# Linear attention into a gated layer: neighbouring heads on the two partition halves, 128-partition loads, and a 136-column product

## The chip, the cores and the metric

One core of one Trainium2 chip runs one launch of the kernel. The metric is the device time of that launch in microseconds (us). With one core there is no second die to compare. The span of a profiled run is some 1.8 us shorter than its time on the clock, so spans are compared with spans and times with times. About 0.15%, or 0.45 us, is the noise between jobs; differences of steady chunks within traces repeat to 0.01 us.

## The reference, cut to what matters

```python
def _attn_ref(q, k, v):                       # each (8 batches, 8 heads, 576, 64), float32
    phi = lambda x: np.where(x > 0, x, np.exp(x) - 1.0) + 1.0
    q_p, k_p = phi(q), phi(k)
    kv  = np.einsum('bhsd,bhse->bhde', k_p, v)
    z   = np.sum(k_p, axis=2)
    num = np.einsum('bhsd,bhde->bhse', q_p, kv)
    den = np.einsum('bhsd,bhd->bhs', q_p, z)[..., None] + 1e-06
    return num / den
# x = attention output as (4608 tokens, 512);  w_in (512, 2048), w_out (2048, 512)
h = x @ w_in;  g = h - np.tanh(h);  out = g @ w_out
```

## The kernel before: the parts that matter

TensorE (PE) does the two large layers in chunks of 512 tokens: layer 1 (16 output tiles x 4 matmuls), then layer 2 (16 groups of 4). The attention of a later batch is threaded in as "steps" after the tiles (`s1`) and the groups (`s2`). Inputs are float32 in HBM; GpSimd's DMAs cast them to bf16.

```python
v_b = [const.tile([128, 2, 3, J, D], BF16) for i in range(2)]   # third "head" is all ones
def load_kq(b, src, store, name):          # batches 1 to 7: two DMAs of 64 partitions
    for hg in range(2) if b > 0 else ():
        nc.gpsimd.dma_start(out=t[64*hg:64*hg+64]..., in_=src[b, 4*hg:4*hg+4]...)
def kv_mm(b, i, ps):                       # per batch 36 matmuls, 64 rows, 192 columns
    nc.tensor.matmul(ps[hg], kp[r, i, j], vt[r, i, :, j, :], ...)   # 2 heads x 64 + 64 ones
attn = Banks([6, 7])                       # numerators alternate between two PSUM banks
def a_num(b, p):                           # numerator of head pair p, then its scaling
    ps = num_mm(b, p, attn)
    nc.vector.tensor_mul(xT[...], ps, rdb[...])
# order of the loads at the start:
#   q0 k0 v0 w_in(4 quarters) k1 q1 | w_out(0) w_out(1) v1 w_out(2)
# steps of batch 1 in chunk 0 (cut):
s1[9]  b0_scale_rest          s1[10] kphi  s1[12] kphi  s1[14] qphi      # layer 1
s2[1]  qphi, load q2, w_out(3), k2, v2     s2[2], s2[3] transposes of qp  # layer 2
s2[4]  prepare   s2[5] kv   s2[7] denominators   s2[8] numerators   s2[10], s2[12] spread
```

"qphi" is an exponential on ScalarE (ACT) and a max and a minimum on VectorE (DVE); its result, qp, is transposed on PE in chunk 0 and by DMA later. "kphi" is the same for k. gT is the gated output of layer 1, made on DVE from the tanh (th) of ACT. xT is the attention output after its scaling by the denominators, the input of layer 1; a "spread" copies the reciprocals of the denominators over the columns that they scale.

## Time and profile before

| | before |
|---|---|
| time, median of 3 runs | 298.7 us |
| span of the profiled run | 297.4 us |
| first matmul of layer 1 | 17.18 us |
| layer 2 of chunk 0 begins | 34.37 us |
| layer 1 of chunk 1 begins | 53.01 us |
| length of chunks 1 to 6, layer 1 to layer 1 | 30.77 us each |

Starts are read from the timeline of PE by line. A chunk's length is the distance between two starts of layer 1.

### The profile page before, as it was taken

How to read it: one execution, taken by the hardware profiler on the slowest of the kernel's cores; microseconds unless marked ns; L12 is line 12 of the kernel's file. 1: busy time of each engine (PE TensorE's matmuls, PEld its weight loads, DVE VectorE, ACT ScalarE, POOL GpSimd, SP SyncE). 2: the span in 40 equal slices, each digit the busy share in tenths (PEclk: the TensorE clock that was granted, in tenths of full speed). 3: DMA queues.
4: the chain of work that ended last, by engine and by line, in shares of the span. 5: the costliest groups of instructions: out<-in, count | busy, mean ns of one | idle time of the engine just before them, and what ended most of it. 6: DMA issues, size and time to landing. Idle time of an engine off the chain costs nothing.

```text
span 297.4 us, 4732 instructions
## 1 busy us (share of the span) xinstructions
PE 286.4 (96%) x1774; PEld 137.3 (46%) x1804; DVE 180.6 (61%) x317; ACT 149.5 (50%) x232; POOL 51.4 (17%) x89
## 2 busy tenths in 40 slices
PE   8898899999999999999999999999999999999994
PEld 3444354454445444544454445444544444444443
DVE  4759858886567764785478547855781468007600
ACT  3747816956444653465347525662562076136421
POOL 8952170240033002400060006000000000000000
PEclk9999999999999999999999999999999999999999
DMA  6999999898969666966797768887108310130033
GB/s 97 187 206 212 205 203 190 157 201 162 232 115 186 144 153 125 182 133 157 153 155 135 171 137 116 149 194 151 37 16 183 72 35 0 37 84 22 2 71 71
DMA packets 39126, 38.95 MB, mean 131 GB/s; under 512 B 16896, under 2 KB 33856, under 8 KB 38336
## 3 DMA queue, kind: packets, MB, share of 16 engines
q0 software_dynamic: 17600, 18.35, 38.8%
q1 hardware_dynamic: 21504, 20.31, 30.4%
q8 instruction: 14, 0.23, 0.3%
q14 instruction: 8, 0.07, 0.1%
HBM read 43.91 MB, written 9.55 MB: 180 GB/s over the span
## 4 chain that ended last, share of the span: by engine, by line
PE 86%; DMA 6%; POOL 5%; issue 1%; ACT 0%; POOLq 0%
PE ps_all L366 40%; PE ps_all L351 37%; DMA w_out_sb<-in_moe_w_out_dram 6%; PE ps_all L179 4%; PE ps_all L302 2%; PE ps_all L559 1%; POOL w_in_sb L113 1%; PE ps_all L259 1%; POOL qraw L88 1%; POOL v L107 1%; POOL kraw L88 1%; POOL v L391 1%; POOL kraw L92 0%; POOL qraw L92 0%; PE ps_all L166 0%
## 5 line engine op out<-in xcount | busy, mean ns | idle before, releaser
L351 PE MATMUL ps_all<-xT,w_in_sb 128*128 128x512 bf16 x560 | 127.3, 379 | 1.9 <-DVE xT L249 0.8
L366 PE MATMUL ps_all<-w_out_sb,gT 128*128 128x512 bf16 x547 | 125.8, 379 | 2.2 <-DMA w_out_sb<-in_moe_w_out_dram 1.3
L357 DVE TENSOR_TENSOR gT<-ps_all,th 128x512 bf16<-128x512 f32 x144 | 96.8, 686 | 50.7 <-ACT th L356 50.1
L356 ACT ACTIVATE th<-ps_all 128x512 f32<-128x512 f32 x144 | 85.0, 598 | 50.1 <-PE ps_all L351 45.2
L351 PEld LDWEIGHTS <-w_in_sb 128*128 128x128 bf16 x576 | 55.1, 98 | 67.6 <-issue 2.2
L366 PEld LDWEIGHTS <-gT 128*128 128x128 bf16 x560 | 54.0, 98 | 65.5 <-issue 1.8
L372 ACT COPY osb<-ps_all 128x512 f32<-128x512 f32 (+1 forms) x37 | 21.2, 573 | 77.5 <-PE ps_all L366 57.8
L313 DVE TENSOR_TENSOR xT<-ps_all,rdb 128x512 bf16<-128x512 f32 x24 | 16.5, 690 | 14.2 <-PE ps_all L302 14.2
L136 ACT ACTIVATE e<-qraw 128x1152 bf16<-128x1152 bf16 x16 | 18.7, 1167 | 4.5 <-DMA qraw<-in_q_dram 4.5
L107 POOL DMA_DIRECT2D v<-in_v_dram x32 | 19.4, 640 | 8.0 <-DMA w_in_sb<-in_moe_w_in_dram 4.0
L362 POOL COPY g<-gT 1x1 bf16<-1x1 bf16 x5 | 0.9, 177 | 111.5 <-DVE gT L357 111.5
L138 DVE TENSOR_TENSOR kp<-e,r 128x1152 bf16<-128x1152 bf16 x15 | 11.4, 758 | 13.3 <-ACT e L136 12.6
L136 ACT ACTIVATE e<-kraw 128x1152 bf16<-128x1152 bf16 x15 | 17.4, 1163 | 0.8 <-DMA kraw<-in_k_dram 0.8
L138 DVE TENSOR_TENSOR qp<-e,r 128x1152 bf16<-128x1152 bf16 x16 | 12.1, 758 | 7.6 <-ACT e L136 6.8
L179 PE MATMUL ps_all<-v,kp 64*128 64x192 bf16 x252 | 11.6, 243 | 0.0
L179 PEld LDWEIGHTS <-kp 64*128 64x128 bf16 x252 | 10.0, 94 | 3.0 <-issue 3.0
L416 PE MATMUL ps_all<-zero 128*128 128x512 bf16 x31 | 9.5, 469 | 1.2 <-DVE zero L379 1.2
L302 PE MATMUL ps_all<-qT,kz 128*128 128x512 bf16 x28 | 10.1, 379 | 0.1
L92 POOL DMA_DIRECT2D qraw<-in_q_dram x14 | 8.7, 639 | 6.2 <-DVE r L137 6.2
L92 POOL DMA_DIRECT2D kraw<-in_k_dram x14 | 8.7, 629 | 4.0 <-issue 2.7
L137 DVE TENSOR_SCALAR r<-qraw 128x1152 bf16<-128x1152 bf16 x16 | 7.5, 466 | 2.4 <-DMA qraw<-in_q_dram 2.4
L188 DVE TENSOR_TENSOR kz<-ps_all,mask 128x320 bf16<-128x320 f32 x14 | 6.2, 484 | 2.5 <-PE ps_all L179 2.5
(73 smaller groups left out, 97.9 us busy)
## 6 DMA issues: line engine op xcount, KB each, us to landing
out_dram<-osb SPq DMA_DIRECT2D x70, 128.0 KB
rdb<-ds SPq DMA_DIRECT2D x12, 576.0 KB
v<-in_v_dram POOLq DMA_DIRECT2D x32, 144.0 KB, 7.8
kraw<-in_k_dram POOLq DMA_DIRECT2D x14, 288.0 KB, 5.2
qraw<-in_q_dram POOLq DMA_DIRECT2D x14, 288.0 KB, 7.3
w_in_sb<-in_moe_w_in_dram POOLq DMA_DIRECT2D x4, 512.0 KB, 10.7
w_out_sb<-in_moe_w_out_dram POOLq DMA_DIRECT2D x4, 512.0 KB, 14.1
qraw<-in_q_dram POOLq DMA_DIRECT2D x4, 144.0 KB, 3.8
```

The costliest lines, as they stand in the source:

```text
L92: nc.gpsimd.dma_start(out=t[64 * hg:64 * hg + 64].rearrange("p i h j d -> p (i h) (j d)"), in_=src[b, 4 * hg:4 * hg + 4].rearrange("h (p j ...
L107: nc.gpsimd.dma_start(out=v_b[b % 2][64 * hg:64 * hg + 64, i, 0:2].rearrange("p h j d -> p h (j d)"), in_=v[b, h0:h0 + 2].rearrange("h (p ...
L136: return (lambda: nc.scalar.activation(e, x, AF.Exp), lambda: nc.vector.tensor_scalar(r, x, 0.0, 1.0, ALU.max, ALU.add), lambda: nc.vector ...
L138: lambda: nc.vector.tensor_tensor(y, e, r, ALU.min))
L179: nc.tensor.matmul(ps[hg], kp[r, i, j].rearrange("p h d -> p (h d)"), vt[r, i, :, j, :], start=(j == 0), stop=(j == J - 1))
L302: nc.tensor.matmul(ps, kz[:, p // 2, p % 2, 0:128], qT[:, p % 2, 0:8, p // 2, :], start=True, stop=True)
L313: nc.vector.tensor_mul(xT[:, p, S * b:S * b + 512].rearrange("p (j t c) -> p j t c", j=8, t=4), ps.rearrange("p j (t c) -> p j t c", t=4), ...
L351: nc.tensor.matmul(h, w_in_sb[:, p, fi * 128:(fi + 1) * 128], xT[:, p, c * 512:(c + 1) * 512], start=(n == 0), stop=(n == NP - 1))
L356: nc.scalar.activation(th, h, AF.Tanh)
L357: nc.vector.tensor_sub(gT[:, fi, :], h, th)
L366: nc.tensor.matmul(o, gT[:, fi, i * 128:(i + 1) * 128], w_out_sb[:, fi, :], start=(fi == 0), stop=(fi == NF - 1))
L372: nc.scalar.copy(osb[:, f0:f1], o[:, f0:f1])
```

## The change

The intent: with heads 2n and 2n+1 on the two partition halves, one DMA of 128 partitions loads what took two of 64. The rows of w_in have to follow. The 64 ones per pair of heads shrink to 8 in a separate tile `vp`, which VectorE fills from v. Chunk 0 is scheduled anew. Its core, with cuts:

```diff
+    kz_c = [const.tile([128, 2, 2, 160], BF16) ...]        # kz no longer from a pool
-    v_b = [const.tile([128, 2, 3, J, D], ...)]
+    v_b = [const.tile([128, 3, 2, J, D], ...)]
+    vp = const.tile([128, 2, J, 136], BF16, name="vp")
+    def load(b, t, src, halves):                            # q, k and v alike
+        x = src[b].rearrange("h (p j) d -> (h p) (j d)", j=J)
+        ... nc.gpsimd.dma_start(out=t..., in_=x.rearrange("(n q) x -> q n x", n=4))
     def load_wi(g):
-        nc.gpsimd.dma_start(out=w_in_sb[:, :, f0:f0 + DF // 4], ... "(ko ki) f -> ki ko f")
+        for h in range(2):
+            nc.gpsimd.dma_start(out=w_in_sb[64*h:64*h+64, ...], ... "(t d) f -> d t f")
+    def a_vp(b, i):
+        nc.vector.tensor_copy(vp[:, i, :, 0:128]..., v_b[b % 2][:, 0:2, i])
+    def a_kv_cols(b, banks):      # as a_kv, with vp[r, i, j, :]: 136 columns
     load_k(1)
+    load_wo(0)
     load_q(1)
-    load_wo(0)
     ...                           # prologue of batch 0: first half of qT, one of two copies moved off ACT;
                                  # second half, both moved onto it; fewer spins (matmuls on zeros)
-            s1[9].append(lambda: b0_scale_rest(first))
-            s1[10] kphi   s1[12] kphi   s1[14] qphi
+            s1[11] kphi   s1[13] kphi   s2[0] qphi
-            s2[2], s2[3] transposes  s2[4] prepare                   s2[5] kv  s2[7] ... s2[12]
+            s2[3], s2[4] transposes  s2[5] b0_scale_rest, prepare    s2[6] kv  s2[8] ... s2[13]
-            s1[...].append(lambda: a_kv(n1, attn))
+            s1[...].append(lambda: (a_kv if c == 1 else a_kv_cols)(n1, attn))
-            s2[d + 6].append(lambda: (a_qphi(n2, 1), a_qT_dma(n2)))
+            s2[d + 6].append(lambda: (a_qphi(n2, 1), a_qT_dma(n2), a_vp(n2, 0), a_vp(n2, 1)))
```

More of the change, by code (lines that the diff above doesn't have):

```diff
@@ L76 @@
     w_out_sb = const.tile([128, NF, DM], BF16, name="w_out_sb")
-    v_b = [const.tile([128, 2, 3, J, D], BF16, name=f"v{i}") for i in range(2)]
+    kz_c = [const.tile([128, 2, 2, 160], BF16, name=f"kz{i}") for i in range(2)]
+    v_b = [const.tile([128, 3, 2, J, D], BF16, name=f"v{i}") for i in range(2)]
+    vp = const.tile([128, 2, J, 136], BF16, name="vp")
     k_t, q_t = {}, {}
-    def load_kq(b, src, store, name):
-        t = kpool.tile([128, 2, 2, J, D], BF16, name=name)
-        for i in range(2) if b == 0 else ():
-            for hg in range(2):
-                h0 = 4 * hg + 2 * i
-                nc.gpsimd.dma_start(
-                    out=t[64 * hg:64 * hg + 64, i].rearrange("p h j d -> p h (j d)"),
-                    in_=src[b, h0:h0 + 2].rearrange("h (p j) d -> p h (j d)", j=J))
-        for hg in range(2) if b > 0 else ():
-            nc.gpsimd.dma_start(
-                out=t[64 * hg:64 * hg + 64].rearrange("p i h j d -> p (i h) (j d)"),
-                in_=src[b, 4 * hg:4 * hg + 4].rearrange("h (p j) d -> p h (j d)", j=J))
-        store[b] = t
+    def load(b, t, src, halves):
+        x = src[b].rearrange("h (p j) d -> (h p) (j d)", j=J)
+        if halves:
+            for i in range(2):
+                nc.gpsimd.dma_start(out=t[:, :, i].rearrange("q h j d -> q h (j d)"),
+                                    in_=x.rearrange("(h i q) x -> i q h x", h=2, i=2)[i])
+        else:
+            nc.gpsimd.dma_start(out=t.rearrange("q h i j d -> q (h i) (j d)"),
+                                in_=x.rearrange("(n q) x -> q n x", n=4))
@@ L97, in load_k @@
     def load_k(b):
-        load_kq(b, k, k_t, "kraw")
+        k_t[b] = kpool.tile([128, 2, 2, J, D], BF16, name="kraw")
+        load(b, k_t[b], k, b == 0)
     def load_q(b):
-        load_kq(b, q, q_t, "qraw")
+        q_t[b] = kpool.tile([128, 2, 2, J, D], BF16, name="qraw")
+        load(b, q_t[b], q, b == 0)
     def load_v(b):
-        for i in range(2):
-            for hg in range(2):
-                h0 = 4 * hg + 2 * i
-                nc.gpsimd.dma_start(
-                    out=v_b[b % 2][64 * hg:64 * hg + 64, i, 0:2].rearrange("p h j d -> p h (j d)"),
-                    in_=v[b, h0:h0 + 2].rearrange("h (p j) d -> p h (j d)", j=J))
+        load(b, v_b[b % 2][:, 0:2], v, b == 0)
@@ L111, in load_wi @@
     def load_wi(g):
         f0 = g * (DF // 4)
-        nc.gpsimd.dma_start(out=w_in_sb[:, :, f0:f0 + DF // 4],
-                            in_=moe_w_in[:, f0:f0 + DF // 4].rearrange("(ko ki) f -> ki ko f", ki=128))
+        for h in range(2):
+            nc.gpsimd.dma_start(out=w_in_sb[64 * h:64 * h + 64, :, f0:f0 + DF // 4],
+                                in_=moe_w_in[256 * h:256 * h + 256, f0:f0 + DF // 4].rearrange(
+                                    "(t d) f -> d t f", d=64))
     def load_wo(g):
@@ L126, in phi_pieces @@
             store[b] = work.tile([128, 2, J, 2, D], BF16, name=name)
-        x = src[b][:, i]
+        x = src[b][:, :, i]
         e = epool.tile([128, 2, J, D], BF16, name="e")
@@ L179, in kv_mm @@
                 nc.tensor.matmul(ps[hg], kp[r, i, j].rearrange("p h d -> p (h d)"),
-                                 vt[r, i, :, j, :], start=(j == 0), stop=(j == J - 1))
+                                 vt[r, :, i, j, :], start=(j == 0), stop=(j == J - 1))
     def a_kv(b, banks):
-        kz_t[b] = work.tile([128, 2, 2, 160], BF16, name="kz")
+        kz_t[b] = kz_c[b % 2]
         ps = [banks()[:, 0:384].rearrange("p (i e) -> p i e", i=2) for hg in range(2)]
@@ L188, in a_kv @@
             nc.vector.tensor_mul(kz_t[b][:, hg], ps[hg][:, :, 0:160], mask[:, hg])
+    def a_vp(b, i):
+        nc.vector.tensor_copy(vp[:, i, :, 0:128].rearrange("p j (h d) -> p h j d", h=2), v_b[b % 2][:, 0:2, i])
+    def a_kv_cols(b, banks):
+        kp = kp_t[b]
+        kz_t[b] = kz_c[b % 2]
+        ps = [banks()[:, 0:272].rearrange("p (i e) -> p i e", i=2) for hg in range(2)]
+        for i in range(2):
+            for j in range(J):
+                for hg in range(2):
+                    r = slice(64 * hg, 64 * hg + 64)
+                    nc.tensor.matmul(ps[hg][:, i, :], kp[r, i, j].rearrange("p h d -> p (h d)"),
+                                     vp[r, i, j, :], start=(j == 0), stop=(j == J - 1))
+        for hg in range(2):
+            nc.vector.tensor_mul(kz_t[b][:, hg, :, 0:136], ps[hg], mask[:, hg, :, 0:136])
     def b0_z(i):
@@ L195, in b0_z @@
                 r = slice(64 * hg, 64 * hg + 64)
-                nc.tensor.matmul(ps_all[:, 4 + 2 * i + hg, 0:32], kp_t[0][r, i, j].rearrange("p h d -> p (h d)"),
+                nc.tensor.matmul(ps_all[:, 4 - 2 * i + hg, 0:32], kp_t[0][r, i, j].rearrange("p h d -> p (h d)"),
                                  one[r, 0:32], start=(j == 0), stop=(j == J - 1))
     def b0_zc(i):
-        nc.vector.tensor_mul(kz_t[0][:, :, i, 128:160], ps_all[:, 4 + 2 * i:6 + 2 * i, 0:32], mask[:, :, i, 128:160])
+        nc.vector.tensor_mul(kz_t[0][:, :, i, 128:160], ps_all[:, 4 - 2 * i:6 - 2 * i, 0:32], mask[:, :, i, 128:160])
     def b0_kv(i):
@@ L207, in b0_kv @@
                 nc.tensor.matmul(ps_all[:, 2 * i + hg, 0:128], kp_t[0][r, i, j].rearrange("p h d -> p (h d)"),
-                                 v_b[0][r, i, 0:2, j, :], start=(j == 0), stop=(j == J - 1))
+                                 v_b[0][r, 0:2, i, j, :], start=(j == 0), stop=(j == J - 1))
     def b0_kz(i):
@@ L350, in l1mm @@
     def l1mm(c, fi, h, p, n):
-        nc.tensor.matmul(h, w_in_sb[:, p, fi * 128:(fi + 1) * 128], xT[:, p, c * 512:(c + 1) * 512],
+        nc.tensor.matmul(h, w_in_sb[:, 2 * (p % 2) + p // 2, fi * 128:(fi + 1) * 128], xT[:, p, c * 512:(c + 1) * 512],
                          start=(n == 0), stop=(n == NP - 1))
@@ L388 @@
     load_k(1)
+    load_wo(0)
     load_q(1)
     for i in (1, 0):
-        nc.gpsimd.memset(v_b[i][:, :, 2], 1.0)
-    load_wo(0)
+        nc.gpsimd.memset(v_b[i][:, 2], 1.0)
+    nc.gpsimd.memset(vp[:, :, :, 128:136], 1.0)
     load_wo(1)
@@ L418 @@
     side = Banks([4, 5, 6, 7])
-    kz_t[0] = work.tile([128, 2, 2, 160], BF16, name="kz")
+    kz_t[0] = kz_c[0]
     (eq0, rq0, mq0), (eq1, rq1, mq1) = (phi_pieces(0, q_t, qp_t, "qp", i) for i in range(2))
-    for f in (eq0, rq0, mq0, eq1, rq1):
+    for f in (eq0, rq0, mq0, eq1, rq1, mq1):
         f()
     spin(18)
-    a_qT_pe(0, 0, side, "AA")
+    a_qT_pe(0, 0, side, "AV")
     (ek0, rk0, mk0), (ek1, rk1, mk1) = (phi_pieces(0, k_t, kp_t, "kp", i, 2 * i) for i in range(2))
-    for f in (mq1, rk0, ek0):
+    for f in (ek0, rk0, *ek1, mk0, rk1):
         f()
-    spin(6)
-    a_qT_pe(0, 1, side, "VV")
-    for f in (*ek1, rk1, mk0):
-        f()
+    spin(5)
+    a_qT_pe(0, 1, side, "AA")
     for t in range(4):
@@ L436 @@
     nc.scalar.copy(sel, s8[:, 0].rearrange("q h p -> q p h").unsqueeze(3).to_broadcast([128, NP, 2, 64]))
-    spin(8)
+    spin(6)
     b0_z(0)
@@ L493, in num1 @@
                     a_num_copy(1, sub["ns"], p, side)
-            s1[9].append(lambda: b0_scale_rest(first))
-            s1[10].append(lambda: a_kphi(1, 0))
-            s1[12].append(lambda: a_kphi(1, 1))
-            s1[14].append(lambda: a_qphi(1, 0))
+            s1[11].append(lambda: a_kphi(1, 0))
+            s1[13].append(lambda: a_kphi(1, 1))
+            s2[0].append(lambda: a_qphi(1, 0))
             s2[1].append(lambda: (a_qphi(1, 1), load_q(2), load_wo(3), load_k(2), load_v(2)))
-            s2[2].append(lambda: a_qT_pe(1, 0, side))
-            s2[3].append(lambda: a_qT_pe(1, 1, side))
-            s2[4].append(prepare)
-            s2[5].append(lambda: a_kv(1, side))
-            s2[7].append(lambda: a_den(1, side))
-            s2[8].append(lambda: (num1(), a_split(1)))
-            s2[10].append(lambda: (spread1(0), a_qphi(2, 0)))
-            s2[12].append(lambda: (spread1(1), a_qphi(2, 1), a_qT_dma(2)))
+            s2[3].append(lambda: a_qT_pe(1, 0, side))
+            s2[4].append(lambda: a_qT_pe(1, 1, side))
+            s2[5].append(lambda: (b0_scale_rest(side), prepare()))
+            s2[6].append(lambda: a_kv(1, side))
+            s2[8].append(lambda: a_den(1, side))
+            s2[9].append(lambda: (num1(), a_split(1)))
+            s2[11].append(lambda: (spread1(0), a_qphi(2, 0)))
+            s2[13].append(lambda: (spread1(1), a_qphi(2, 1), a_qT_dma(2)))
             s2[15].append(lambda: a_kphi(2, 0))
         elif n1 < B:
-            s1[6 if c == 1 else 5].append(lambda: a_kv(n1, attn))
+            s1[6 if c == 1 else 5].append(lambda: (a_kv if c == 1 else a_kv_cols)(n1, attn))
             s1[9 if c == 1 else 8].append(lambda: (a_den(n1, attn), a_spread(n1)))
@@ L522 @@
             s2[d + 4].append(lambda: a_qphi(n2, 0))
-            s2[d + 6].append(lambda: (a_qphi(n2, 1), a_qT_dma(n2)))
+            s2[d + 6].append(lambda: (a_qphi(n2, 1), a_qT_dma(n2), a_vp(n2, 0), a_vp(n2, 1)))
         if c == 0:
-            first = Banks([4, 5, 6, 7, 0, 1, 2, 3, 2, 4, 5, 6, 7])
+            first = Banks([4, 5, 6, 7, 0, 1, 2, 3])
             hs = [ps_all[:, n, :] for n in range(4)]
```

## The prediction

> **What bounds the kernel now.** I read the page's head first, then the chain of waits, the PE waits, the stretch table, and single timelines.
>
> ```profile
> PE 286.4 (96%) x1774; PEld 137.3 (46%) x1804; DVE 180.6 (61%) x317; ACT 149.5 (50%) x232; POOL 51.4 (17%) x89
> ...
> DMA  6999999898969666966797768887108310130033
> ...
> PE 86%; DMA 6%; POOL 5%; issue 1%; ACT 0%; POOLq 0%
> ```
>
> TensorE is busy 286.4 of 297.4 us, and the chain that ended last is 86% PE. But the DMA row is at 9 from the second slice to the eighth: for the first 55 us the transfers are as full as PE. So there are two kernels in one: a start (0 to 53 us) where DMA and PE take turns, and a steady part where only PE counts. The stretch table (columns: PE, PEld, DVE, ACT, POOL busy; clock; DMA share; GB/s written) says so.
>
> ```profile
> 8.00:10.00 2.00, 1.50 (x11) 0.53 (x8) 1.28 (x3) 2.00 (x4) 2.00 (x4) 1.00 1.16 191
> 10.00:12.00 2.00, 2.00 (x16) 1.06 (x15) 1.82 (x5) 1.94 (x4) 2.00 (x4) 1.00 1.21 191
> ...
> 18.00:20.00 2.00, 2.00 (x24) 1.05 (x21) 1.28 (x2) 0.00 (x0) 0.00 (x0) 1.00 1.27 204
> 20.00:25.00 5.00, 5.00 (x25) 2.29 (x24) 3.35 (x6) 3.80 (x7) 1.35 (x2) 1.00 1.23 209
> 25.00:30.00 5.00, 4.19 (x23) 1.90 (x23) 4.35 (x8) 3.13 (x5) 1.73 (x3) 1.00 1.21 212
> ...
> 35.00:53.00 18.00, 17.63 (x153) 9.05 (x155) 12.78 (x32) 8.42 (x13) 5.58 (x9) 1.00 1.17 198
> ...
> 145.50:176.30 30.80, 30.64 (x186) 14.57 (x188) 20.49 (x33) 16.12 (x24) 5.02 (x9) 1.00 0.78 152
> ```
>
> A steady chunk takes 30.8 us with 0.16 us of PE idle: a nanosecond off PE there is a nanosecond off the kernel, and a new PE wait costs its full length. After the prologue PE waits little either:
>
> ```profile
> PE ps_all L366 <- DMA w_out_sb<-in_moe_w_out_dram: 1.3, 1, 1.3
> PE ps_all L351 <- DVE xT L249: 0.8, 1, 0.8
> ```
>
> **What the Trainium skill says.** "SBUF — State Buffer", Door 1: The DMA port swizzle: 64 partitions reach 8 of 16 ports and measured 196 GB/s at 1 MiB, against 328 for 128 partitions; this is presumably why the change was made. The trace does not bear it out here: the loads cast float32 to bf16, so written bytes are half the bytes read, and k and v of batch 0, 64 partitions each, were written at 191 GB/s (8 to 12 us), w_in at 128 partitions at 204 to 209, k and q of batch 1 at 64 partitions at 212. "DMA: Bandwidth & Descriptors", Rules for kernel authors, says two transfers to disjoint halves share the same 16 engines; that fits. "TensorE: Matmul & The Clock Gate", Back-to-back issue gap: warm, N/2.4 + 2.5 ns per matmul; the pairs below agree. "VectorE: DVE Perf Modes", The perf-mode tier table, puts bf16 tensor_copy and tensor_scalar in one 4x tier; so the new copies should cost what the tensor_scalar of the same 1152 elements costs (452 ns in the trace).
>
> **Part 1: kv with 136 columns instead of 192 (batches 3 to 7).** The v tile carried 64 ones per pair of heads, though the denominator needs a few columns. The timelines give 64x128 and 64x192 matmuls:
>
> ```profile
> 12.62 0.66 PE L207 MATMUL ps_all<-v,kp 64*128 64x128 bf16 x18
> ...
> 40.64 1.66 PE L179 MATMUL ps_all<-v,kp 64*128 64x192 bf16 x36
> ```
>
> Two row halves run together, so 18 matmuls are 9 pairs. Taking the last matmul's own time off: (660 - 216)/8 = 56 ns per pair at 128 columns, (1660 - 243)/17 = 83 ns at 192: 0.43 ns a column. At 136 columns about 59 ns. 18 pairs x 24 ns = 0.43 us a batch, 5 batches: **-2.1 us**, all on PE, all in stretches without PE slack.
>
> **Part 2: the copies into vp.** Two VectorE copies of 128x1152 bf16 a batch, 0.45 to 0.54 us each with spacing: 0.9 to 1.0 us, five times. VectorE has 10 us idle a chunk, so the sum is harmless; the place is not. They sit behind the last qp minimum and ahead of the first scaling of the numerators, and those numerators live in two PSUM banks:
>
> ```profile
> 139.33 0.76 DVE L138 TENSOR_TENSOR qp<-e,r 128x1152 bf16<-128x1152 bf16 x1 [1.11 <-ACT e L136]
> 140.00 1.36 DVE L313 TENSOR_TENSOR xT<-ps_all,rdb 128x512 bf16<-128x512 f32 x2
> ...
> 139.18 0.38 PE L302 MATMUL ps_all<-qT,kz 128*128 128x512 bf16 x1
> ...
> 140.25 0.38 PE L302 MATMUL ps_all<-qT,kz 128*128 128x512 bf16 x1
> ...
> 141.33 0.38 PE L302 MATMUL ps_all<-qT,kz 128*128 128x512 bf16 x1
> ```
>
> The third numerator (141.33) takes the bank that the first scaling must have read. That scaling now starts at 140.00. With 0.95 us of copies ahead it starts at 140.95, ends 0.69 later at 141.64; with some 0.06 us of signalling PE goes at 141.70: a new PE wait of about 0.37 us. It arises where copies and numerators are neighbours, in chunks 2 to 5 (in chunk 1 the numerators come two steps later): 4 x 0.37 = **+1.5 us** (0.6 to 2 for copies of 0.35 to 0.55 us).
>
> **Part 3: the loads at the start.** Twelve DMAs of 144 KB become six of 288 KB; w_in goes from four to eight. An issue takes about 0.63 us of GpSimd whether it covers 128 or 256 rows of the source, so q, k and v are issued in 6 x 0.64 instead of 12 x 0.64 us, 3.8 us less; w_in gives back about 4 x 0.65 = 2.6 less a little. But the queue is already backlogged: the first packets run at 2.5 us, and the k issued at 5.4 lands 5.7 us later. Bytes ahead of any weight stay equal. What is left is that q's first half is one request (it landed at 4.3 and 5.0 in two), with perhaps a better ramp (135 GB/s at 4 to 6 us against 191 later): I allow 0.5 us on all landings of the prologue, 0 to 1.2. The ACT and VectorE reordering (one qT copy moved off ACT before the k exponentials) does not win more by itself: the first w_in lands at 9.6 + 7.3 = 16.9 us, and the first L1 matmul ran at 17.2. So L1 starts near 16.5.
>
> **Part 4: the weights of chunk 0.** The first w_out quarter is moved ahead of q of batch 1. It landed at 17.2 + 17.2 = 34.4 us, where PE waited 1.3 us; 590 KB of written bf16 ahead of it at about 200 GB/s are 2.9 us, so it lands at about 31. The 0.8 us wait on xT (the rest of batch 0, moved into the second layer) goes too. L1 takes 64 x 0.216 = 13.8 us plus 0.5, so layer 2 starts near 31 instead of 34.4. But then PE runs into what comes next: q of batch 1, now behind, lands near 34, so its transposes can't run before 36; and the later quarters of w_out keep their place in the queue:
>
> ```profile
> 38.76 0.77 POOL L117 DMA_DIRECT2D w_out_sb<-in_moe_w_out_dram  x1
> ...
> DMA to landing us min/median/max: 9.3/9.3/9.3
> ```
>
> The last quarter landed at 38.8 + 9.3 = 48.1 us, and the step that needs it began at 49.4, after the spread at 48.2: only 1.3 us of slack. With everything 0.5 us earlier it lands at 47.6, when PE also arrives (second quarter at 36.4, then eight steps of 0.86 plus transposes, kv, denominators, numerators and spread, 4.3 us: 47.6). Four steps and one spread later, 3.9 us, layer 1 of chunk 1 begins at 51.5 against 53.2: **-1.7 us**, not the 3.4 that the start of layer 2 suggests.
>
> **Sum:** -2.1 + 1.5 - 1.7 = -2.3; I shade it to -2.6 for a better ramp: 298.7 - 2.6 = 296.1 us, 0.9% down.
>
> **The rivals.** (a) The 128-partition loads really are faster, as the port table says: then the eight DMA-full slices shrink, chunk 0 gains 4 us or more, and the time is 293 to 294. For it: the slow 4 to 8 us, all 64-partition loads. Against it: the 212 GB/s of later 64-partition loads, and w_in, which goes the other way. (b) The copies cause no PE wait (they are faster, or the minimum ahead comes earlier): then -2.1 - 1.7 gives 294.9. For it: only that the margin is small; against it the bank arithmetic above. (c) The copies run in a slower mode (0.76 us, as the minimum does): a wait of 1 us in four chunks, +4, and with -3.8 elsewhere the time stays near 299. (d) Chunk 0 gains nothing because the later q of batch 1 stalls the transposes and ACT, which carries the exponentials, the tanh and the copies in one order: the time is 298. ACT was busy all of 30 to 35 us, which speaks for some of it.
>
> **Range and chances.** The kv term is sure to 0.3 us; the copies' wait could be 0 to 4 us, chunk 0 could give 0 to 4 us. Combined, 8 in 10 lie in 293.8 to 298.2. Faster by 2% needs 292.7 or less, that is both rival a and rival b: 6%. Slower by 2% (304.7) has no mechanism: 1%. Within 2%: 93%.
>
> **What would show it.** A kv group of 64x136 matmuls near 1.2 us per 36; two copies near 0.45 us each; a PE wait on the scaling of xT of some 0.4 us in four chunks (none there means rival b); the first layer-1 matmul near 16.5 us and layer 2 of chunk 0 near 31; the last w_out quarter landing near 47.6 with PE waiting for it or just arriving; chunk 1 beginning near 51.5. Wrong would be: landings more than 1.5 us earlier throughout (a), or layer 1 still starting at 17 or later.

## The result, and the profile after

The changed kernel took 295.61 us (median of 4 runs, 295.37 to 295.89), the kernel before 298.86 us in 4 runs. The ratio is 0.9892, 95% interval 0.9875 to 0.9909. Ratios throughout are the mean time of one kernel's runs over that of the other's in the same rounds, so they are not quite the ratio of the medians quoted. That is 3.25 us less; 2.6 were predicted.

The head of the page after, against the one in the prediction:

```profile
PE 285.9 (97%) x1801; PEld 134.9 (46%) x1801; DVE 182.3 (62%) x326; ACT 150.4 (51%) x233; POOL 31.9 (11%) x53
...
DMA  6999999898959665957697679776117310230033
...
PE 91%; DVE 3%; DMA 3%; POOL 1%; issue 1%; ACT 0%; DVEq 0%; POOLq 0%
```

Before, GpSimd (POOL) stood at 51.4 us and 89 instructions; fewer DMAs bring it to 31.9 and 53, and its share of the chain that ended last falls from 5% to 1%. The DMA row is unchanged over the first 50 us. In that chain, DVE has come in with 3%. The waits of PE in the first 60 us (us in total, times, longest) lead to these DVE links:

```profile
PE ps_all L165 <- DVE qp L137: 1.2, 2, 0.6
PE ps_all L432 <- DVE zero L394: 1.2, 1, 1.2
PE ps_all L222 <- DMA v<-in_v_dram: 0.5, 1, 0.5
PE ps_all L366 <- DVE xT L245: 0.3, 1, 0.3
```

The two waits of before (1.3 us for w_out, 0.8 us for xT) are gone. A wait of transposes on qp has taken their place; of its two, one belongs to batch 0 at 7.7 us, and only 0.6 us to chunk 0. The chain from 29 to 35.8 us runs through DVE: products gT, both minima of k, then qp. The PE timeline of chunk 0 after shows the place:

```profile
31.59 3.62 PE L381 MATMUL ps_all<-w_out_sb,gT 128*128 128x512 bf16 x16
35.80 0.68 PE L165 MATMUL ps_all<-ident,qp 128*128 128x128 bf16 x9 [0.59 <-DVE qp L137]
...
51.12 2.10 PE L366 MATMUL ps_all<-xT,w_in_sb 128*128 128x512 bf16 x9
```

Layer 2 starts at 31.59 instead of 34.37, four groups (16 matmuls) run, PE waits for qp, and chunk 1 begins at 51.12 instead of 53.01. The later gain is in the products (groups of the page by line: busy us, mean ns) and in the steady stretch, whose PE idle is now rounded to nothing:

```profile
L200 PE MATMUL ps_all<-vp,kp 64*128 64x136 bf16 x180 | 6.2, 220 | 0.0
L190 DVE COPY vp<-v 128x1152 bf16<-128x1152 bf16 x10 | 4.1, 453 | 0.0
...
82.00:112.40 30.40, 30.40 (x192) 14.09 (x188) 21.29 (x36) 16.11 (x24) 2.40 (x4) 1.00 0.80 154
```

The busy sums would say 6.2/5 = 1.24 us a batch against 11.6/7 = 1.66: 0.42 us each. All times of the two profiled runs together:

| | before | after | difference |
|---|---|---|---|
| layer 1 begins | 17.18 | 16.94 | -0.24 |
| chunk 0, from there to layer 1 of chunk 1 | 35.83 | 34.18 | -1.65 |
| chunk 1 | 30.78 | 30.78 | 0 |
| chunks 2 to 5, each | 30.77 | 30.49 | 4 x -0.28 |
| chunk 6 | 30.77 | 30.36 | -0.41 |
| span | 297.4 | 294.0 | -3.4 |

Chunk 6 has the short product but no copies, chunks 2 to 5 have both: 0.41 us won, some 0.14 us given back. A timeline of chunk 2 after (DVE first, then PE) shows how:

```profile
106.25 0.76 DVE L137 TENSOR_TENSOR qp<-e,r 128x1152 bf16<-128x1152 bf16 x1 [1.10 <-ACT e L135]
106.92 0.82 DVE L190 COPY vp<-v 128x1152 bf16<-128x1152 bf16 x2
107.66 1.88 DVE L328 TENSOR_TENSOR xT<-ps_all,rdb 128x512 bf16<-128x512 f32 x3
```

```profile
106.09 0.38 PE L317 MATMUL ps_all<-qT,kz 128*128 128x512 bf16 x1
...
107.17 0.38 PE L317 MATMUL ps_all<-qT,kz 128*128 128x512 bf16 x1
...
108.39 0.38 PE L317 MATMUL ps_all<-qT,kz 128*128 128x512 bf16 x1
...
109.47 0.38 PE L317 MATMUL ps_all<-qT,kz 128*128 128x512 bf16 x1
```

Numerators come 1.08 us apart, except the third: 1.22 us, 0.14 too late. The first scaling began at 107.66 and took 0.69 us, so it ended at 108.35, and the third numerator, which needs its bank, began at 108.39. The profile does not list this as a wait, since PE is still counted busy with the tail of the matmuls before; only the spacing shows it.

### The profile page after: what moved, and what is told of

It is laid out like the page before. It is cut to its first block, busy times and chain, and to the rows that moved or that the text cites. A ratio compares the mean times of both kernels' runs of the same rounds, so it can differ in the third digit from the quotient of the medians.

```text
span 294.0 us, 4681 instructions
## 1 busy us (share of the span) xinstructions
PE 285.9 (97%) x1801; PEld 134.9 (46%) x1801; DVE 182.3 (62%) x326; ACT 150.4 (51%) x233; POOL 31.9 (11%) x53
## 3 DMA queue, kind: packets, MB, share of 16 engines
q1 hardware_dynamic: 21504, 20.31, 30.6%
## 4 chain that ended last, share of the span: by engine, by line
PE 91%; DVE 3%; DMA 3%; POOL 1%; issue 1%; ACT 0%; DVEq 0%; POOLq 0%
PE ps_all L366 42%; PE ps_all L381 40%; DMA v<-in_v_dram 3%; PE ps_all L317 2%; PE ps_all L200 2%; PE ps_all L572 1%; PE ps_all L178 1%; DVE gT L372 1%; PE ps_all L274 1%; DVE kp L137 1%; PE ps_all L241 1%; POOL kraw L90 0%; POOL qraw L90 0%; PE ps_all L222 0%; PE ps_all L165 0%
## 5 line engine op out<-in xcount | busy, mean ns | idle before, releaser
L381 PE MATMUL ps_all<-w_out_sb,gT 128*128 128x512 bf16 x560 | 128.1, 379 | 0.0
L328 DVE TENSOR_TENSOR xT<-ps_all,rdb 128x512 bf16<-128x512 f32 x24 | 15.8, 686 | 11.7 <-PE ps_all L317 11.7
L432 PE MATMUL ps_all<-zero 128*128 128x512 bf16 x29 | 8.6, 454 | 1.2 <-DVE zero L394 1.2
L285 DVE RECIPROCAL rden<-den 128x144 f32<-128x144 f32 x7 | 7.4, 1053 | 0.2
L136 DVE TENSOR_SCALAR r<-kraw 128x1152 bf16<-128x1152 bf16 x15 | 6.8, 451 | 0.1
L93 POOL DMA_DIRECT2D qraw<-in_q_dram x7 | 5.2, 748 | 14.6 <-DVE r L136 13.4
L200 PEld LDWEIGHTS <-kp 64*128 64x128 bf16 x180 | 5.3, 94 | 2.1 <-issue 2.1
L200 PE MATMUL ps_all<-vp,kp 64*128 64x136 bf16 x180 | 6.2, 220 | 0.0
L93 POOL DMA_DIRECT2D kraw<-in_k_dram x7 | 5.2, 749 | 3.7 <-issue 1.3
```

The lines of the kernel that those rows point to most:

```text
L93: nc.gpsimd.dma_start(out=t.rearrange("q h i j d -> q (h i) (j d)"), in_=x.rearrange("(n q) x -> q n x", n=4))
L136: lambda: nc.vector.tensor_scalar(r, x, 0.0, 1.0, ALU.max, ALU.add),
L200: nc.tensor.matmul(ps[hg][:, i, :], kp[r, i, j].rearrange("p h d -> p (h d)"), vp[r, i, j, :], start=(j == 0), stop=(j == J - 1))
L328: nc.vector.tensor_mul(xT[:, p, S * b:S * b + 512].rearrange("p (j t c) -> p j t c", j=8, t=4), ps.rearrange("p j (t c) -> p j t c", t=4), ...
L381: nc.tensor.matmul(o, gT[:, fi, i * 128:(i + 1) * 128], w_out_sb[:, fi, :], start=(fi == 0), stop=(fi == NF - 1))
```

## The experiments

My theory before the first runs: the steady part gives 1.5 us (shorter products less the bank wait), chunk 0 and its start give the rest, by order and schedule and not by the width of the loads. The main rival: the 128-partition loads do it.

### Products of 192 columns again

```diff
- s1[...]: (a_kv if c == 1 else a_kv_cols)(n1, attn)     s2[d+6]: ..., a_vp(n2, 0), a_vp(n2, 1)
+ s1[...]: a_kv(n1, attn)                                s2[d+6]: ...
```

> The changed kernel with the 136-column product and its two copies taken out again (all batches multiply the 192-column tile, as before). My theory: of the 3.25 us won, the steady part gives 5 x 0.42 us of shorter products less 4 x 0.14 us of a new PE wait, 1.5 us; so this kernel is 1.5 us slower than the changed one, about 297.1 us, ratio to before 0.994, with steady chunks of 30.77 us and chunk 1 still beginning near 51.3 us. Rival: the steady part wins nothing and all comes from the start; then 295.6 us, ratio 0.989.

Measured: 297.19 us (5 runs), ratio 0.9945 (0.9931 to 0.9958); chunks 1 to 6 are 30.77 us again, and chunk 1 begins at 51.03. Against the changed kernel that is 1.6 us. The steady part's share is settled, and 1.6 us are left for the start. In this profiled run PE waited 0.43 us for the last w_out quarter (landed at 47.2), and chunk 0 took 34.67 us; nothing in the edit touches that load.

### Copies behind the last numerator

```diff
- s2[d+6]: a_qphi(n2, 1), a_qT_dma(n2), a_vp(n2, 0), a_vp(n2, 1)
+ s2[d+6]: a_qphi(n2, 1), a_qT_dma(n2)      s2[14]: a_vp(n2, 0)      s2[15]: a_vp(n2, 1)
```

> The changed kernel with the two vp copies moved behind the last numerator of the chunk. Theory: the copies delay the first scaling of the numerators, so the third numerator waits for its PSUM bank (0.14 us in chunks 2 to 5); without them ahead the wait goes, 0.56 us less in all: 295.0 us, ratio 0.987, third numerator 1.08 us after the second. Rival: the spacing has another cause (the copies are free); then 295.6 us and the gap of 1.22 us stays.

Measured: 294.67 us (4 runs), ratio 0.9863 (0.9849 to 0.9876). Chunks 2 to 5 are 30.36 us, and the numerators are 1.08 us apart throughout. The DVE timeline of chunk 2 now reads:

```profile
105.74 0.76 DVE L137 TENSOR_TENSOR qp<-e,r 128x1152 bf16<-128x1152 bf16 x1 [1.10 <-ACT e L135]
106.42 1.36 DVE L328 TENSOR_TENSOR xT<-ps_all,rdb 128x512 bf16<-128x512 f32 x2
...
110.56 0.82 DVE L190 COPY vp<-v 128x1152 bf16<-128x1152 bf16 x2
```

The same two copies, at a place where DVE has nothing to do for PE, cost nothing. The chunks account for 4 x 0.14 = 0.56 us; the 0.9 us between the medians contain the noise between jobs.

### The copies twice

```diff
- s2[d+6]: ..., a_vp(n2, 0), a_vp(n2, 1)
+ s2[d+6]: ..., a_vp(n2, 0), a_vp(n2, 1), a_vp(n2, 0), a_vp(n2, 1)
```

> The changed kernel with the two vp copies done twice at the same place (the second pair rewrites the same values). Theory: two more copies at 0.37 us spacing push the first scaling back 0.74 us, and since the slack is already used up, the third numerator waits all of it, in chunks 2 to 5: 4 x 0.74 = 3.0 us more, 298.6 us, ratio 0.999. Rival: VectorE has 9 us idle a chunk, so copies cost nothing: 295.6 us.

Measured: 298.59 us (4 runs), ratio 0.9995 (0.9981 to 1.0008). Chunks 2 to 5 take 31.23 us, 0.74 more than in the changed kernel, chunk 1 is unchanged. Now the wait is long enough to be listed:

```profile
140.14 0.38 PE L317 MATMUL ps_all<-qT,kz 128*128 128x512 bf16 x1 [0.72 <-DVE xT L328]
```

VectorE is idle for about a third of a chunk, and yet 0.74 us of work in the wrong place costs 0.74 us each time, 4 x 0.74 = 3.0 us: nearly all of the change's gain.

### Loads of q, k and v by 64 partitions, everything else as changed

```diff
- nc.gpsimd.dma_start(out=t.rearrange("q h i j d -> q (h i) (j d)"), in_=x.rearrange("(n q) x -> q n x", n=4))
+ for g in range(2):            # same tiles, same rows, same order
+     nc.gpsimd.dma_start(out=t[64*g:64*g+64]..., in_=...)
```

> The changed kernel with every load of q, k and v cut in two DMAs of 64 partitions each, same tiles, same order, same bytes. My theory: PE is not waiting for these transfers in the changed kernel but for one DMA of v (0.5 us) and for qp; 64 or 128 partitions moves the landings by some 0.3 us, so 295.6 to 296.1 us, ratio 0.989 to 0.991. Rival (the 128-partition loads are what makes the start faster): the landings of the later weights slip back by the 1.2 to 1.6 us that they came earlier, and the time is 297 us or more, ratio 0.994 or more.

Measured: 296.06 us (4 runs), ratio 0.9913 (0.9899 to 0.9926). Next to the changed kernel's two series (295.61 and 295.22) that is 0.45 to 0.85 us. The last w_out quarter lands at 38.2 + 9.3 = 47.4 us, against 37.4 + 9.1 = 46.5 with 128 partitions. So the wide loads do make the landings about 0.9 us earlier, but most of this is not on PE's path: what reaches it is qp, for which PE now waits 0.9 us instead of 0.6. The rival's 1.4 us or more are refuted; my "0 to 0.5 us" was at its upper edge. The edit makes the DMAs twice as many as well as narrower, and the run does not tell the two apart.

### w_in by four DMAs of 128 partitions (wrong result on purpose)

```diff
- for h in range(2): nc.gpsimd.dma_start(out=w_in_sb[64*h:64*h+64, ...], ...)
+ nc.gpsimd.dma_start(out=w_in_sb[:, :, f0:f0 + DF // 4], ... "(ko ki) f -> ki ko f")
```

> The changed kernel with w_in loaded by four DMAs of 128 partitions again instead of eight of 64. Rows then meet the wrong tokens, so the result is wrong on purpose; times and traces are those of a valid kernel. My theory: w_in is not waited for once the first quarter is there, and 64 partitions are no slower here; 295.6 us give or take 0.4, ratio 0.988 to 0.991. Rival (64 partitions cost w_in bandwidth): 128 partitions are faster, 294.9 us or less, w_in landing 1 us or more earlier.

Measured: 295.68 us (4 runs), ratio 0.9896 (0.9875 to 0.9917); the result is wrong, as intended. The quarters of w_in land at 16.1, 19.5, 22.0 and 24.6 us; in halves of 64 partitions the later halves landed at 16.6, 19.4, 22.0 and 24.4. The first quarter is whole 0.5 us earlier, but the first matmul of layer 1 waits for xT and not for it; the later quarters agree within 0.2 us. For w_in, partition width makes no difference to the time that a run here shows.

### The w_out quarter behind q again

```diff
- load_k(1); load_wo(0); load_q(1)
+ load_k(1); load_q(1); load_wo(0)
```

> The changed kernel with the first w_out quarter behind q of batch 1 again, as before. Layer 2 of chunk 0 then begins when that quarter lands, near 33.2 us instead of 31.6. Theory: the two orders trade one wait for another: with q early, PE no longer waits 1.2 us for qp at the transposes, so only 0.4 us of the 1.6 us reach the end: 296.0 us, ratio 0.990. Rival: the order of these two loads carries the gain of chunk 0, and all 1.6 us come back: 297.2 us, ratio 0.9945.

Measured: 297.04 us (6 runs, 296.71 to 298.55), ratio 0.9956 (0.9933 to 0.9979). My 0.4 us is wrong. Two things had gone into it. First, I had read 1.2 us of waiting for qp off the list shown above, of which only 0.6 belongs to chunk 0; with the right figure 1.6 - 0.6 = 1.0 us is expected, and the four runs at full clock (296.71 to 297.11) show 1.1 to 1.5 over 295.61, or 1.5 to 1.9 over the 295.22 of the changed kernel's second series. The rival's 1.6 us fits no worse. The trade itself did not happen either. q landed at 30.6 us instead of 33.1, but qp came no earlier, as DVE shows (the changed kernel first, then this run):

```profile
33.23 1.28 DVE L372 TENSOR_TENSOR gT<-ps_all,th 128x512 bf16<-128x512 f32 x2
...
34.98 0.76 DVE L137 TENSOR_TENSOR qp<-e,r 128x1152 bf16<-128x1152 bf16 x1
```

```profile
34.45 0.76 DVE L137 TENSOR_TENSOR qp<-e,r 128x1152 bf16<-128x1152 bf16 x1
```

Layer 1 began at 16.94 and at 16.41, so the minimum that makes qp starts 18.04 us later in both. It stands behind DVE's own queue, the products gT and the minima of k, and not behind q. PE no longer waits for qp only because layer 2 starts later. Second, in two of the six runs (298.27 and 298.55, mean granted clock 0.994) something else happened, which the stretches of the profiled one show (length; PE, PEld, DVE, ACT, POOL busy; granted PE clock; DMA share; GB/s):

```profile
32.00:33.00 1.00, 0.00 (x0) 0.00 (x0) 0.98 (x2) 1.00 (x2) 0.00 (x0) 1.00 1.26 210
33.00:34.00 1.00, 0.83 (x3) 0.35 (x4) 1.00 (x3) 1.00 (x2) 0.00 (x0) 0.65 1.24 210
34.00:35.00 1.00, 1.00 (x4) 0.37 (x3) 0.90 (x2) 0.55 (x1) 0.00 (x0) 0.50 1.24 204
35.00:36.00 1.00, 1.00 (x3) 0.30 (x2) 0.90 (x3) 0.00 (x0) 0.00 (x0) 0.50 1.20 207
36.00:37.00 1.00, 1.00 (x4) 0.40 (x3) 0.44 (x1) 0.00 (x0) 0.89 (x2) 0.65 1.21 208
```

PE stood idle for 1.95 us, waiting for w_out; when it resumed, its clock was halved for about 3.4 us (the four clock figures, 0.65, 0.50, 0.50 and 0.65, lack 1.7 us of full clock together). That put 1.7 us on top of the wait itself: the first 16 matmuls of layer 2 took 5.31 us, against 3.62 in the changed kernel. The 1.33 us that PE waited for w_out in the kernel before had left the clock at 1.00. The Trainium skill, "TensorE: Matmul & The Clock Gate" (What's actually happening), describes such a gate: half clock after an idle window of about 3.4 us, with windows that run freely. This trace agrees in the factor and in the length, but an idle time of 1.95 us was enough.

### The kernel before with only the order of the loads

```diff
- load_k(1); load_q(1); memsets; load_wo(0)
+ load_k(1); load_wo(0); load_q(1); memsets
```

> The kernel before with one part of the change: the first w_out quarter ahead of q of batch 1. Theory: layer 2 of chunk 0 starts 1.3 us earlier (33.0), but q lands near 34.4 and PE waits for qp at the transposes instead; 0.4 us are left: 298.4 us, ratio 0.9985. Rival: 1.3 us won, 297.5 us, ratio 0.9955.

Measured: 298.77 us (6 runs), ratio 1.0002 (0.9987 to 1.0017). The 1.3 us for w_out are gone from PE's waits, and the time has not moved: not even the 0.4 us can be seen, though in the profiled run chunk 1 begins 0.35 us earlier (52.66), after a layer 1 that began 0.54 us later. The rival's 1.3 us are refuted.

### The order, and the rest of batch 0 in layer 2

```diff
+ the edit above
- s1[9]: b0_scale_rest(first)        s2[4]: prepare
+                                    s2[4]: b0_scale_rest(side), prepare     # and a shorter list of banks for layer 1
```

> The kernel before with two parts of the change: the w_out quarter ahead of q of batch 1, and the rest of batch 0 (last 64 columns of xT) moved from layer 1 into layer 2. Theory: layer 1 ends 0.8 us earlier and layer 2 starts near 32.2, but the transposes still wait for qp near 36.4, and the moved product costs its 0.4 us there: 298.4 to 298.8 us, ratio 0.9985 to 1.000. Rival: the waits add up and all 2.1 us (1.3 + 0.8) are won: 296.7 us, ratio 0.993.

Measured: 298.85 us (6 runs), ratio 1.0004 (0.9989 to 1.0018). Both waits of before (2.1 us) have been removed and nothing has been won. The PE timeline says what took their place:

```profile
31.78 2.75 PE L366 MATMUL ps_all<-w_out_sb,gT 128*128 128x512 bf16 x12
35.93 0.68 PE L166 MATMUL ps_all<-ident,qp 128*128 128x128 bf16 x9 [1.39 <-DVE qp L138]
...
37.76 0.68 PE L166 MATMUL ps_all<-ident,qp 128*128 128x128 bf16 x9 [0.29 <-DVE qp L138]
```

Layer 2 starts 2.6 us earlier (31.78), but after three groups stand the transposes, and qp is not there before 35.9. That q lands later in this order (second half at 33.9 instead of 31.8) explains little of it: DVE lost 0.30 us to it just before qp, and its minimum for qp began at 35.11, against 35.30 in the kernel before. The rest is mostly DVE's own queue, as above.

### The order and the whole schedule of chunk 0, on the kernel before

```diff
+ the two edits above
- s1[10] kphi  s1[12] kphi  s1[14] qphi   s2[2], s2[3] transposes  s2[5] kv  s2[7] ... s2[12]
+ s1[11] kphi  s1[13] kphi  s2[0]  qphi   s2[3], s2[4] transposes  s2[6] kv  s2[8] ... s2[13]
```

> The kernel before (64-partition loads, old tiles, 192 columns) with only the schedule of chunk 0 taken from the change: w_out quarter ahead of q, rest of batch 0 in layer 2, and every step of batch 1 one place later, so that four groups of layer 2 run ahead of the transposes instead of three, and the q exponentials follow the last tanh. Theory after the runs b1 and b3: this shift is what turns the two removed waits into time, because the transposes wait for qp near 36 us anyway and one more group (0.86 us) fits ahead of it; chunk 1 begins near 51.5 us, 297.4 us, ratio 0.9955 (range 0.994 to 0.997). Rival: without the 128-partition loads the schedule wins nothing; 298.7 us, ratio 1.000.

Measured: 297.92 us (5 runs), ratio 0.9968 (0.9955 to 0.9980), inside the expected range and not at its middle. Chunk 0 takes 34.19 us, as long as with the whole change (34.18):

```profile
32.15 3.62 PE L366 MATMUL ps_all<-w_out_sb,gT 128*128 128x512 bf16 x16
36.36 0.68 PE L166 MATMUL ps_all<-ident,qp 128*128 128x128 bf16 x9 [0.59 <-DVE qp L138]
...
37.74 0.67 PE L166 MATMUL ps_all<-ident,qp 128*128 128x128 bf16 x9
```

One more group, 16 matmuls instead of 12, stands ahead of the transposes; it fills 0.86 us of the wait, and the second transposes wait no more: with the q exponentials behind the last tanh, DVE makes both halves of qp one after the other, without a product in between. With old tiles, old loads and old products, a third of the change's gain is there.

### The copies on GpSimd

```diff
- nc.vector.tensor_copy(vp[:, i, :, 0:128]..., ...)
+ nc.gpsimd.tensor_copy(vp[:, i, :, 0:128]..., ...)
```

> The changed kernel with the vp copies on GpSimd instead of VectorE, at the same place in the program. Theory: VectorE's numerators are no longer behind the copies, so the steady chunk is 30.36 us as in the run with late copies: 294.9 us, ratio 0.987. Rival: the GpSimd copies slow VectorE where both read SBUF, and the chunk stays at 30.5 us or more.

Measured: 295.00 us (4 runs), ratio 0.9868 (0.9853 to 0.9883); chunks 2 to 5 are 30.36 us. The theory holds, although a copy takes 1.15 us on GpSimd instead of 0.45. In the same job the changed kernel gave 295.22, so 0.2 of the 0.56 us in the chunks is seen in the medians; the rest is within the scatter of the start.

### A version meant to beat both

```diff
+ copies behind the last numerator, as above
- s1[...]: (a_kv if c == 1 else a_kv_cols)(n1, attn)      s2[15] of chunk 0: a_kphi(2, 0)
+ s1[...]: a_kv_cols(n1, attn)                            s2[15] of chunk 0: a_kphi(2, 0), two a_vp(2) on GpSimd
```

> A version meant to beat both: the changed kernel with the copies behind the last numerator, and batch 2 by the 136-column product as well (its two copies on GpSimd, which is idle then). Theory: 0.42 us less than the late copies alone, 294.3 us, ratio 0.985, with chunk 1 at 30.36 us instead of 30.77. Rival: the GpSimd copies of batch 2 come too late for the product, or hold back the loads of batch 3; then 294.7 us or more.

Measured: 294.96 us (4 runs), ratio 0.9867 (0.9853 to 0.9880). In the profiled run chunk 1 takes 30.36 us, and all six chunks do, as the theory said; but its chunk 0 takes 34.64 us, with a PE wait of 0.4 us for the last w_out quarter, which landed at 47.4. Nothing in the edit touches the loads before it, and the run with 192 columns again shows the same wait (0.43 us, landing at 47.2), so it seems to go with the run and not with this version; two profiled runs do not settle it. The version is faster than the kernel before and not shown faster than the simpler one with late copies (294.67).

### The changed kernel once more

> The changed kernel as it is, once more, as the yardstick for the runs beside it: 295.6 us, ratio 0.989.

Measured: 295.22 us (4 runs), ratio 0.9877 (0.9863 to 0.9890). It is the yardstick for the three runs before.

## Why the prediction was right, point by point

The time was predicted at 296.1, in 293.8 to 298.2; it came out at 295.6. Faster by more than 2% did not occur. That the sum came so near is partly luck: 0.3 of the 2.6 us were a shade "for a better ramp", while what the sum of -2.3 lacked was mainly an error in part 2. A slip in reading: the DMA row stands at 9 from the second slice to the seventh, not the eighth.

- **Part 1, the product: right in mechanism and size.** Predicted 59 ns a pair and 2.1 us in all. The chain of waits has 1.17 us per 36 matmuls where it had 1.59, and 5 x 0.42 = 2.1 us; undoing it with its copies lost 1.6 us, as 2.1 - 0.56 asks.
- **Part 2, the copies: right in mechanism, and the term was too large.** The step was "+1.5 us" from a wait of 0.37 us in four chunks; measured were 0.14 us in exactly those chunks, 0.56 us. What was mis-sized is the delay of the first scaling: 0.95 us for two copies of 0.45 to 0.54 us. Each copy does last 453 ns, but the second starts 0.37 us after the first, and the delay is 0.74 us. Even the low end of the range given for this term, 0.6 us, lies just above the 0.56. The doubled copies confirm that here, once the slack of 0.6 us is used up, each further copy costs its spacing: 0.74 us for two more. These 0.94 us are the largest single error, larger than the 0.65 us by which the sum was off.
- **Part 3, the loads: the sum near, the reason wrong.** Layer 1 was to start near 16.5; it did at 16.94 in the profiled run, and between 16.34 and 16.80 in eight other profiled runs with the new prologue and wide loads. The old prologue lies between 17.13 and 17.72 in four runs. With the new prologue and 64-partition loads it is 16.86, so the width is not shown to be what starts layer 1 earlier. The step that failed is the limit: the first matmul of layer 1 was to wait for w_in, but in every profiled run it waits for xT of batch 0 (0.3 us), with w_in landed before (16.6 in the changed kernel). There the chain runs back from xT to v of batch 0, which landed at 12.35. Nor did the loads speed up in the way assumed: q's first half landed later (5.6 against 5.0 us). The DMAs moved less from 3 to 4 us (86 against 164 GB/s), and more from 4 to 6 us (206 against 135). An issue of 288 or 576 KB took about 0.75 us where 0.64 was counted. The prediction's allowance of 0.5 us for all landings was too small later on (1.6 us for the last w_out quarter), which did not matter.
- **Part 4, chunk 0: the time right (51.3 in the chain of waits against 51.5 predicted), both of its limits wrong in part.** Layer 2 at 31 (measured 31.6) and the transposes at 36 (35.8) came as told, but the transposes not for the reason told: q was to hold them back, and the run with q ahead of w_out shows that q 2.5 us earlier leaves qp where it was, behind DVE's queue. The last w_out quarter was to land just as PE needed it, at 47.6; it landed at 46.5, PE arrived at about 47.4 and waited for nothing. In two other profiled runs with the new schedule it landed at 47.2 and 47.4, and PE waited 0.4 us, so this limit is near. In the changed kernel, what keeps the earlier layer 2 from passing on its whole 2.8 us is qp. The three runs on the kernel before show this: two waits removed are worth nothing until another group is put ahead of the transposes. Nor does the shift pay alone: the changed kernel with the old order of the two loads lost 1.1 to 1.5 us at full clock. The prediction counted the new order of steps without naming that shift as the thing that pays.
- **The rivals.** (a) is refuted by the loads of 64 partitions (0.45 to 0.85 us lost) and by w_in of 128 (no difference). (b) is refuted by the spacing of the numerators, though the truth lies nearer to it than to my term. (c) fell with the 453 ns, (d) with the 1.65 us of chunk 0; but an engine that does its work in one order does hold qp back, only it is DVE with products and minima, and not ACT.

As an estimate from the runs, the parts add up: 1.5 us of the steady part, 1.0 of order and schedule on the kernel before, and 0.45 to 0.85 of the wide loads are 3.0 to 3.4 of the 3.25 us. The new prologue (the moved qT copies, w_in in halves) was not run alone; what it is worth is not shown.

What stays open: why landings of the later weights gain 1.2 to 1.6 us in full, of which cutting q, k and v in halves takes back about 0.9; and whether the scatter of the start, some 0.6 us between profiled runs of like kernels, has a cause within the kernel.

## What to carry to other kernels

A wait taken away in front of an in-order engine is worth only what the engine can do until its next wait: find that next wait first, and move independent work ahead of it together with the fix. Small helper work on an engine with plenty of idle time still costs whatever exceeds the slack where it stands ahead of the operation that frees a PSUM bank (here 0.74 us of copies against 0.6 us of slack); put it behind that operation. A wait on a tile names the last link only: before blaming the load behind it, see what else its engine had to do first. And when a waiting table sums several places under one line, look at each place before using the sum.

## What the Trainium skill lacked or had wrong

- "SBUF — State Buffer", Door 1: its figures for 64 against 128 partitions (196 and 328 GB/s at 1 MiB) do not carry over to these casting loads from HBM, many of them queued: 206 GB/s written in all at 20 to 25 us, with the halved w_in of the changed kernel, 209 with the full-width w_in of the kernel before. Cutting q, k and v in halves cost 0.45 to 0.85 us in all.
- "TensorE: Matmul & The Clock Gate", What's actually happening: it speaks of an idle window of about 3.4 us. Here PE ran at half clock for about 3.4 us after 1.95 us of idle time, in one profiled run, and the clock record of a second of six runs is alike.
- "VectorE: DVE Perf Modes", Two Vector instructions with no wait between them: it models when the next instruction is held, without a figure for how far two that are not held overlap. Here two copies of 128x1152 bf16, 453 ns each, started 0.37 us apart; sizing them by their duration made the prediction's term too large.
